# Second expert part of a three-part kernel: its ScalarE, VectorE and GpSimd operations in a written-out order, transposes into tiles of their own, low products of an output later

## The chip, the cores and the metric

The kernel runs on one core of one Trainium2 chip. The metric is the device time of one execution in microseconds (us). The profile gives times from the start of its own span, which is some 2 us shorter than the device time of the same execution.

## The reference

A linear attention with decay feeds two dense expert layers; the second one has a softmax and a layer norm inside. The part that the change touches is the second layer.

```
attn_out = _attn_ref(q, k, v)                 # (4, 8, 768, 64), decayed running state
x = attn_out as (3072 tokens, 512)
# first expert layer, d_ff = 2048
h = x @ w_in;  g = h - tanh(h);  x = g @ w_out
# second expert layer, d_ff = 1024
h = x @ w_in2
e = exp(h - max(h));  sm = e / (sum(e) + 1e-9)
solu = h * sm
mu = mean(solu);  var = mean((solu - mu)**2)
ln = (solu - mu) / sqrt(var + 1e-6) * g_ln
out = ln @ w_out2
```

## The kernel before

All matrix products are made in a high and a low part: an operand is cast to a reduced format (the high part), the rest (the low part) is a difference, and TensorE multiplies high by high, high by low and low by high. So each operand costs a cast on ScalarE (L160) and a difference on VectorE or GpSimd (L161, L475).

Tokens are handled in tiles of 128. The second layer takes 12 pairs of tiles, `Pair(0)` to `Pair(11)`; tile `2j+1` is called a here and tile `2j` b. A pair's first product is made with seven block products instead of eight, in the order P1, P2, P6, P5, P7, P4, P3 (`Pair.part`), each of 6 matmuls (L925). Between them ScalarE copies partial sums out of PSUM (`keep2`, L932, tiles `part`); P6 and P7 go on in the bank of P1 and so wait for the copy before them. VectorE makes the halves of a tile's hidden row from a bank and a copy, with a running maximum (`add_half`, L940): a's are complete after P4, b's after P3.

Then each tile goes through `soft`: exp on ScalarE (L950), weighting with the hidden row and its sum on VectorE (L952, called weigh here; the mean is a small operation behind it, L953), subtraction of the mean on ScalarE (L954, center), squares on ScalarE (L956), a transpose in 32x32 blocks on VectorE (L958), and small operations for the scale (L961 to L967, the last two on GpSimd). The transposed tile is written to DRAM (`ud`, L959) and read back in another order into `hn` (L972, `turn`); so the transpose across partitions is completed. `trans` splits that tile into `uh` and `ul` (L160, L161). `outp` makes the second product, 24 matmuls (L989) of `uh` and `ul` with the eight decoded pieces of w_out2, and evicts it with the scale (L993).

In the last stretch `pair_of(j, j-1)` makes pair j's seven products, and `outs(j-1)` the two outputs of the pair before it. Pair 10 has no outputs behind it: pair 11 follows at once, then the outputs of pairs 9, 10 and 11. Pair 0's products lie between the last products of the first layer (`products_y`, L377, 12 matmuls for each of 16 steps f; the operands of step f are `gp`, split by `split_p(f)` with L160 and L161); pair 0's P3 comes behind step 11, and steps 12 to 15 follow it. This place is called the changeover here.

Who sets the order: TensorE's instructions stand as the program writes them (`tc.manual_schedule`). Those of ScalarE, VectorE and GpSimd are placed by the scheduler of the framework, which also puts in the semaphores; `pin` keeps an instruction in the order of the program. SP's loads of `hn` and writes of `ud` are pinned. Tiles of 4 KB a partition come from one pool of 40 (`t4`); the transpose is written over `ex`.

Of the kernel before, what the change touches and what calls it, by code (L numbers as in the profile page):

```python
# [47 lines left out]
LATER = 3  # L48
LOADS = 3
# [39 lines left out]
def body(ctx: ExitStack, tc, z, w_in, w_out, w_in2, w_out2, g_ln, cst, tab, out):  # L89
# [67 lines left out]
    P1, P2, P6, P5, P7, P4, P3 = range(7)  # L157

    def parts(h, o, src, eng):
        nc.scalar.copy(h, src)  # L160
        eng.tensor_tensor(o, src, h.bitcast(F32), ALU.subtract)  # L161
# [309 lines left out]
    def on_pool(n, out, a, b, op):  # L471
        k = out.shape[1] // n
        for i in range(n):
            at = slice(i * k, (i + 1) * k)
            nc.gpsimd.tensor_tensor(out[:, at], a[:, at], b[:, at], op)  # L475

    def sum_y(j):
        t = yl[j]
        a11, a12, a21, a22 = (t[:, i, k : k + 2, :] for i in range(2) for k in (0, 2))
        s = ysum[j] = t4([P, 4, 2, P], F32, "ysum")  # L480
        s1, s2, s3, s4 = (s[:, i, :, :] for i in range(4))
        nc.gpsimd.tensor_tensor(s1, a21, a22, ALU.add)
        nc.gpsimd.tensor_tensor(s2, s1, a11, ALU.subtract)
        nc.gpsimd.tensor_tensor(s3, a11, a21, ALU.subtract)
        nc.gpsimd.tensor_tensor(s4, a12, s2, ALU.subtract)

    def split_y(j, halves=(0, 1)):
        flat = "p a k t -> p (a k t)"
        for g in halves:
# [11 lines left out]
            for lo, n, src in todo:  # L501
                h, o = (w[:, lo : lo + n, :, :].rearrange(flat) for w in y)
                nc.scalar.copy(h, src)  # L503
                on_pool(n, o, src, h.bitcast(F32), ALU.subtract)
# [425 lines left out]
    def keep2(ph):  # L930
        t = t2([P, 512], F32, "part")
        nc.scalar.copy(t, ph)  # L932
        return t
# [4 lines left out]
    def add_half(h, half, ph, part, seen):  # L938
        hn, nm = h
        nc.vector.tensor_tensor_reduce(  # L940
            hn[:, half * 512 : (half + 1) * 512], ph, part, -1.0,
            3.0e38 if seen is None else nm[seen], ALU.add, ALU.min, nm[half],
        )

    def soft(i, h, last):

        hn, nmx = h[0], h[1][last]
        ex = t4([P, FF2], F32, "ex")
        ssum = sp.tile([P, 1], F32, tag="ssum", name="ssum")
        nc.scalar.activation(ex, hn, AF.Exp, bias=nmx, scale=-1.0, accum_out=ssum)  # L950
        us = sp.tile([P, 1], F32, tag="us", name="us")
        nc.vector.scalar_tensor_tensor(ex, hn, 1.0, ex, ALU.mult, ALU.mult, accum_out=us)  # L952
        nc.vector.tensor_scalar(us, us, -1.0 / FF2, None, ALU.mult)  # L953
        nc.scalar.activation(hn, ex, AF.Identity, bias=us)  # L954
        ssq = sp.tile([P, 1], F32, tag="ssq", name="ssq")
        nc.scalar.activation(ex, ex, AF.Square, bias=us, accum_out=ssq)  # L956

        nc.vector.transpose(ex, hn)  # L958
        pin(nc.sync.dma_start(out=ud[i], in_=ex))  # L959

        nc.vector.tensor_scalar(ssum, ssum, 1e-9, -1.0, ALU.add, ALU.mult)  # L961
        nc.vector.reciprocal(ssum, ssum)
        nc.vector.tensor_scalar(ssq, ssq, ssum, ssum, ALU.mult, ALU.mult)
        nc.vector.tensor_scalar(ssq, ssq, 1.0 / FF2, 1e-6, ALU.mult, ALU.add)
        sc = sp.tile([P, 1], F32, tag="sc", name="sc")
        nc.gpsimd.tensor_tensor(sc, ssq, mhalf, ALU.pow)
        nc.gpsimd.tensor_tensor(sc, sc, ssum, ALU.mult)  # L967
        uc[i], sc2[i] = hn, sc
# [8 lines left out]
    def trans(i):  # L977
        u = uc.pop(i)
        uh, ul = (t4([P, NF2 * P], F32R, "u" + n) for n in "hl")
        parts(uh, ul, u, nc.vector)  # L980
        ut[i] = [w.rearrange("p (f t) -> p f t", f=NF2) for w in (uh, ul)]

    def outp(i):
        uh, ul = ut.pop(i)
        po = ps_o.tile([P, DM], F32, tag="o", name="po")
        for f in range(NF2):
            bh, bl = dec2.w[f]
            for n, (a, b) in enumerate(((uh, bh), (uh, bl), (ul, bh))):
                nc.tensor.matmul(  # L989
                    po, a[:, f, :], b, start=f == 0 and n == 0, stop=f == NF2 - 1 and n == 2  # L990
                )
        ob = t2([P, DM], F32, "ob")
        nc.scalar.activation(ob, po, AF.Copy, scale=sc2.pop(i))  # L993
        at = i % B * S + i // B * P
        nc.scalar.dma_start(out=out[at : at + P, :], in_=ob)

    class Pair:
# [5 lines left out]
        def part(self, m):  # L1003
# [20 lines left out]
            elif m == P4:  # L1024
# [3 lines left out]
                soft(2 * j + 1, self.a, 0)  # L1028
            else:
                product2(j, P3, self.q3, False)  # L1030
                add_half(self.b, 1, self.q3, self.u2, 0)
                soft(2 * j, self.b, 1)
# [6 lines left out]
    for n, (s, f) in enumerate(steps):  # L1039
# [19 lines left out]
        if s == NSB - 1:  # L1059
# [13 lines left out]
            for m in {8: (P1, P2), 9: (P6, P5), 10: (P7, P4), 11: (P3,)}.get(f, ()):  # L1073
                pair.part(m)
            if f == 9:
# [15 lines left out]
    def pair_of(j, before):  # L1091
        pair = Pair(j)
        for n, m in enumerate((P1, P2, P6, P5, P7, P4, P3)):
            if n == 5 and before is not None:
                trans(2 * before + 1)
            pair.part(m)
            if n in (0, 2) and j + 1 < NJ:
                split_y(j + 1, (n // 2,))
            if n == 4 and j + 2 < NJ:
                sum_y(j + 2)  # L1100
            if n == 4 and j + 3 < NJ:
                load_y(j + 3)
        turn(j)
        if before is not None:
            trans(2 * before)

    def outs(j, after=None):
        for half in (1, 0):
            outp(2 * j + half)
            if after is not None:  # L1110
                trans(2 * after + half)

    with tc.manual_schedule(engines={mybir.EngineType.PE}):
        for j in range(1, NJ - 1):
            pair_of(j, j - 1)
            if j < NJ - 2:
                outs(j - 1)
        pair_of(NJ - 1, None)
        outs(NJ - 3, NJ - 2)
        outs(NJ - 2, NJ - 1)  # L1120
# [60 lines left out]
```

## Time and profile before

| | |
|---|---|
| median of 3 executions | 853.78 us (853.65 to 854.4) |
| profiled execution, its own time | 853.42 us |
| its span | 851.5 us |
| share of the span that matmuls are busy | 96% |
| share that VectorE, ScalarE, GpSimd are busy | 63%, 55%, 34% |

The time is the median of the unprofiled executions; the profile shows one execution more, which took 853.42 us. Shares are of the whole span, over stages that have different limits; what an edit is worth has to be read in its own stage.

### The profile page before, as it was taken

To read this page: it belongs to the slowest core of one execution; us is meant where nothing else is said; L and a number is where in the kernel's file an instruction comes from. 1 tells how busy PE (TensorE), PEld (TensorE's weight loads), DVE (VectorE), ACT (ScalarE), POOL (GpSimd) and SP (SyncE) were. 2 spreads that over 40 slices of the span, in tenths; PEclk is the share of its full clock that TensorE was granted. 3 is DMA by queue.
4 is the path that set the end of the run, shared out by engine and by line. 5 is a ranking of instruction groups with operands and counts; after the bars stand their busy time and mean duration, and the time that the engine had idled before them with its cause. 6 is when DMAs were issued, how large, how long until landed. Compare 5 with 4: busy or idle time off the path is not lost.

```text
span 851.5 us, 16381 instructions
## 1 busy us (share of the span) xinstructions
PE 820.1 (96%) x6296; PEld 672.9 (79%) x6296; DVE 536.0 (63%) x999; ACT 468.2 (55%) x880; POOL 291.2 (34%) x304
## 2 busy tenths in 40 slices
PE   5699999999999999999999999999999999999998
PEld 4678888788877777888788888888888888888876
DVE  3778985999867948322662897483555555555561
ACT  4546753656456546444562446354666666666672
POOL 4511200090635329344400260064444444444310
PEclk8899999999999999999999999999999999999999
DMA  9658854353899825963592818380787667776675
GB/s 359 248 205 292 289 201 129 123 183 108 308 366 329 301 77 175 399 263 128 196 366 94 313 44 309 112 283 26 149 173 149 149 149 148 149 149 123 124 173 99
DMA packets 168461, 169.42 MB, mean 199 GB/s; under 512 B 105664, under 2 KB 117952, under 8 KB 168384
## 3 DMA queue, kind: packets, MB, share of 16 engines
q1 hardware_dynamic: 160032, 153.38, 59.5%
q10 hardware_dynamic: 8352, 15.00, 4.9%
q8 instruction: 49, 0.80, 0.4%
q14 instruction: 28, 0.23, 0.1%
HBM read 107.02 MB, written 61.34 MB: 198 GB/s over the span
## 4 chain that ended last, share of the span: by engine, by line
PE 84%; DVE 5%; DMA 4%; issue 3%; ACT 2%; POOL 1%; SPq 0%; ACTq 0%; DVEq 0%; POOLq 0%
PE py L377 30%; PE ph L753 16%; PE po L989 14%; PE ph L352 10%; PE ph L925 10%; PE out L228 3%; PE sc L228 2%; DVE ul L161 1%; DMA z<-z 1%; DVE hn L940 1%; DMA raw<-w_in 1%; DMA wcd<-wch 1%; ACT part L932 1%; DMA hn<-ud 1%; POOL hs L771 0%
## 5 line engine op out<-in xcount | busy, mean ns | idle before, releaser
L377 PE MATMUL py<-gp,w 128*128 128x512 f32 x768 | 175.1, 389 | 0.0
L377 PEld LDWEIGHTS py<-gp,w 128*128 128x128 f32 x768 | 144.1, 188 | 30.0
L989 PE MATMUL po<-w,uh 128*128 128x512 f32 x384 | 118.5, 390 | 0.0
L771 POOL TENSOR_TENSOR hs<-hs,th 128x512 f32<-128x512 f32 x48 | 66.5, 1389 | 96.1 <-ACT th L769 84.0
L989 PEld LDWEIGHTS po<-w,uh 128*128 128x128 f32 x384 | 72.1, 188 | 14.8
L352 PE MATMUL ph<-xh,w 128*128 128x512 f32 x256 | 83.1, 399 | 0.0
L377 PE MATMUL py<-gh,w 128*128 128x512 f32 x256 | 79.2, 390 | 0.3 <-ACT gh L365 0.3
L989 PE MATMUL po<-w,ul 128*128 128x512 f32 x192 | 75.9, 395 | 2.9 <-DVE ul L161 2.5
L153 ACT CAST w<-wf 128x512 fp32r<-128x512 f32 x70 | 43.1, 621 | 55.9 <-DVE wf L144 46.1
L940 DVE CUSTOM_DVE_ANT_0 hn<-ph,part 128x512 f32<-128x512 f32 x24 | 16.6, 691 | 82.0 <-ACT part L932 46.8
L769 ACT ACTIVATE th<-hs 128x512 f32<-128x512 f32 x48 | 30.3, 631 | 61.5 <-DVE hs L779 54.9
L154 DVE TENSOR_TENSOR w<-wf,w 128x512 fp32r<-128x512 f32 x70 | 51.1, 734 | 14.4 <-ACT w L153 13.6
L161 DVE TENSOR_TENSOR gp<-g,gp 128x512 fp32r<-128x512 f32 x64 | 48.2, 764 | 18.5 <-ACT gp L160 18.4
L925 PE MATMUL ph<-w,yhs 128*128 128x512 f32 x192 | 59.2, 390 | 0.2 <-ACT part L932 0.2
L753 PE MATMUL ph<-xh,wch 128*128 128x512 f32 x140 | 57.1, 408 | 1.6 <-DVE hs L779 1.6
L352 PEld LDWEIGHTS ph<-xh,w 128*128 128x128 f32 x256 | 48.6, 190 | 11.1 <-DVE w L154 0.4
L377 PEld LDWEIGHTS py<-gh,w 128*128 128x128 f32 x256 | 48.0, 188 | 10.6 <-ACT gh L365 0.7
L160 ACT CAST gp<-g 128x512 fp32r<-128x512 f32 x64 | 38.6, 618 | 30.8 <-DMA g<-gd 18.4
L753 PE MATMUL ph<-xl,wch 128*128 128x512 f32 x140 | 55.3, 395 | 0.0
L779 DVE TENSOR_TENSOR hs<-ph,part 128x512 f32<-128x512 f32 x48 | 32.9, 686 | 35.3 <-PE ph L753 22.9
L753 PE MATMUL ph<-xh,wcl 128*128 128x512 f32 x140 | 55.1, 394 | 0.0
L475 POOL TENSOR_TENSOR yla<-yl,yha 128x256 fp32r<-128x256 f32 x36 | 27.7, 797 | 78.7 <-ACT yha L503 78.7
(123 smaller groups left out, 1788.0 us busy)
## 6 DMA issues: line engine op xcount, KB each, us to landing
z<-z SPq DMA_DIRECT2D x48, 512.0 KB, 6.5
g<-gd SPq DMA_DIRECT2D x64, 256.0 KB, 5.3
raw<-w_in SPq DMA_DIRECT2D x24, 512.0 KB, 6.7
raw<-w_out SPq DMA_DIRECT2D x24, 512.0 KB, 4.5
gd<-hs SPq DMA_DIRECT2D x48, 256.0 KB, 3.5
ud<-ex SPq DMA_DIRECT2D x24, 512.0 KB, 3.1
hn<-ud SPq DMA_DIRECT2D x24, 512.0 KB, 6.9
y1d<-ysb SPq DMA_DIRECT2D x24, 256.0 KB, 3.6
```

Source lines behind the costliest of these rows:

```text
L153: pin(nc.scalar.copy(hi, wf), fixed)
L154: pin(eng.tensor_tensor(lo, wf, hi.bitcast(F32), ALU.subtract), fixed)
L160: nc.scalar.copy(h, src)
L161: eng.tensor_tensor(o, src, h.bitcast(F32), ALU.subtract)
L228: pin(nc.tensor.matmul(o, a, b, start=True, stop=True, skip_group_check=True), held[0])
L352: nc.tensor.matmul(ph, a[:, k, :], x, start=n == 0, stop=n == 3 * NK - 1), s < 2
L377: nc.tensor.matmul(py[e], a[:, cols], x, start=f == 0 and n == 0, stop=f == NF1 - 1 and n == 2)
L753: nc.tensor.matmul(ph, a, x, start=first and n == 0, stop=n == 5, skip_group_check=True)
L771: eng.tensor_tensor(g, h, th, ALU.subtract)
L779: nc.vector.tensor_tensor(h, ph, part, ALU.add)
L925: nc.tensor.matmul(ph, x[:, r, :], w, start=first and n == 0, stop=n == 5, skip_group_check=True)
L989: nc.tensor.matmul(po, a[:, f, :], b, start=f == 0 and n == 0, stop=f == NF2 - 1 and n == 2)
```

## The change

`fix` pins an instruction from the place on where `late[0]` is set, ahead of pair 1: from there on the operations of ScalarE, VectorE and GpSimd in the second layer stand as the program writes them. `soft` is cut into five steps (`Soft`), which `pair_of` and `outs` call at chosen places. The transpose goes into a tile of its own, `ut`. `trans` is cut into `high` (cast) and `low` (difference). In `outp` the low product of piece f comes `LAG` = 3 pieces later. The last output is evicted in two halves, one on ScalarE and one on VectorE, with two stores.

```
 LATER = 3
+LAG = 3
...
+    late = [False]
+
+    def fix(ins):
+        pin(ins, late[0])
...
+    class Soft:
+
+        def __init__(self, i, h, last):
+            self.i, self.hn, self.nm = i, h[0], h[1][last]
+
+        def exp(self):
...
+        def weigh(self):
...
+        def center(self):
+            fix(nc.scalar.activation(self.hn, self.ex, AF.Identity, bias=self.us))
+
+        def turn(self):
+            t = t4([P, FF2], F32, "ut")
+            fix(nc.vector.transpose(t, self.hn))
+            pin(nc.sync.dma_start(out=ud[self.i], in_=t))
+            uc[self.i] = self.hn
+
+        def norm(self):
+            ssq, ssum = sp.tile([P, 1], F32, tag="ssq", name="ssq"), self.ssum
+            fix(nc.scalar.activation(self.ex, self.ex, AF.Square, bias=self.us, accum_out=ssq))
...
-        for f in range(NF2):
-            bh, bl = dec2.w[f]
-            for n, (a, b) in enumerate(((uh, bh), (uh, bl), (ul, bh))):
...
+        todo = []
+        for f in range(NF2 + LAG):
+            if f < NF2:
+                todo += [(uh, f, 0), (uh, f, 1)]
+            if f >= LAG:
+                todo.append((ul, f - LAG, 0))
...
+        if i == NTT - 2:
+            l, r = slice(0, DM // 2), slice(DM // 2, DM)
+            fix(nc.scalar.activation(ob[:, l], po[:, l], AF.Copy, scale=sc))
+            fix(nc.vector.tensor_scalar(ob[:, r], po[:, r], sc, None, ALU.mult))
...
+                if m in (P4, P3):
+                    u = pair.sa if m == P4 else pair.sb
+                    u.weigh()
+                    u.center()
+                    u.turn()
+                    u.norm()
...
-    def pair_of(j, before):
+    def pair_of(j, before=None):
+
+        a, b = (None, None) if before is None else (2 * before + 1, 2 * before)
         pair = Pair(j)
         for n, m in enumerate((P1, P2, P6, P5, P7, P4, P3)):
-            if n == 5 and before is not None:
-                trans(2 * before + 1)
             pair.part(m)
-            if n in (0, 2) and j + 1 < NJ:
-                split_y(j + 1, (n // 2,))
...
+            if n < 2 and j + 1 < NJ:
+                split_y(j + 1, (n,))
+            if n == 2 and a is not None and j > 1:
+                high(a)
+                low(a)
+            if n == 4:
+                if a is not None:
+                    if j > 1:
+                        high(b)
+                    else:
+                        high(a)
+                        low(a)
...
+        for u in (pair.sa, pair.sb):
+            u.weigh()
+        if a is not None and j == 1:
+            high(b)
+        pair.sa.center()
+        pair.sa.turn()
+        if a is not None:
+            low(b)
+        pair.sb.center()
+        pair.sb.turn()
         turn(j)
...
+    late[0] = True
     with tc.manual_schedule(engines={mybir.EngineType.PE}):
...
+        for j in range(1, NJ - 2):
+            pair = pair_of(j, j - 1)
+            outs(j - 1, pair)
+        pair = pair_of(NJ - 2, NJ - 3)
+        pair.sa.norm()
+        pair.sb.norm()
+        pair = pair_of(NJ - 1)
+        outs(NJ - 3, pair, NJ - 2)
+        outs(NJ - 2, None, NJ - 1)
         outs(NJ - 1)
```

What the built programs hold at three places follows (line numbers are each program's own).

ScalarE at the changeover, from pair 0's first exp on: before, `gp` being the casts of steps 13, 14 and 15 of the first layer.

```order
L950 ACTIVATE ex,ssum<-hn,nm 128x1024
L160 CAST gp<-g 128x512
L954 ACTIVATE hn<-ex,us 128x1024
L950 ACTIVATE ex,ssum<-hn,nm 128x1024
L160 CAST gp<-g 128x512 x2
L153 CAST w<-wf 128x512
```

The same place in the change.

```order
L958 ACTIVATE ex,ssum<-hn,nm 128x1024
L970 ACTIVATE hn<-ex,us 128x1024
L980 ACTIVATE ex,ssq<-ex,us 128x1024
L165 CAST gp<-g 128x512
L958 ACTIVATE ex,ssum<-hn,nm 128x1024
L970 ACTIVATE hn<-ex,us 128x1024
L980 ACTIVATE ex,ssq<-ex,us 128x1024
L165 CAST gp<-g 128x512 x2
L154 CAST w<-wf 128x512
```

Tile a's center and squares now stand ahead of the cast of step 13, and tile b's exp, center and squares ahead of those of steps 14 and 15. On VectorE each difference `gp` stands behind the same tile's transpose and scale operations; before, it stood ahead of them.

VectorE in a pair of the middle, from the addition of tile a's first half on: before (`ISA hn` are the additions, `ul` the low products of the pair before).

```order
L940 ISA hn,nm<-ph_7212,part,nm 128x512
L940 ISA nm 128x1
L161 TENSOR_TENSOR ul<-hn,uh 128x1024
L940 ISA hn,nm<-ph_7183,part,nm 128x512
L940 ISA nm 128x1
L952 SCALAR_TENSOR_TENSOR ex,us<-hn,ex 128x1024
```

The same pair in the change, from one addition earlier.

```order
L1003 TENSOR_TENSOR ul<-hn,uh 128x1024
L945 ISA hn,nm<-ph_7148,part 128x512
L945 ISA nm 128x1
L945 ISA hn,nm<-ph_7219,part,nm 128x512
L945 ISA nm 128x1
L945 ISA hn,nm<-ph_7191,part,nm 128x512
L945 ISA nm 128x1
L964 SCALAR_TENSOR_TENSOR ex,us<-hn,ex 128x1024
L967 TENSOR_SCALAR us<-us 128x1
```

The low product of tile a moved from behind the third addition to ahead of the second; that of tile b now stands between the two transposes, where before it followed the second weigh.

ScalarE from pair 10's first exp to pair 11's copies: before (`part` are pair 11's copies of P1, P6, P5 and P7).

```order
L950 ACTIVATE ex,ssum<-hn,nm 128x1024
L932 COPY part<-ph_8762 128x512
L950 ACTIVATE ex,ssum<-hn,nm 128x1024
L160 CAST uh<-hn 128x1024
L954 ACTIVATE hn<-ex,us 128x1024
L932 COPY part<-ph_8762 128x512
L956 ACTIVATE ex,ssq<-ex,us 128x1024
L932 COPY part<-ph_8787 128x512
```

The same place in the change.

```order
L958 ACTIVATE ex,ssum<-hn,nm 128x1024 x2
L970 ACTIVATE hn<-ex,us 128x1024 x2
L980 ACTIVATE ex,ssq<-ex,us 128x1024 x2
L937 COPY part<-ph_8784 128x512 x2
L937 COPY part<-ph_8809 128x512
```

The copy of pair 11's P1, which stood between pair 10's two exps, now stands behind both exps, both centers and both squares.

## Rows read from the trace of the kernel before

**Rows 1.** Page, part 1: busy time, share of the span, instructions.

```profile
PE 820.1 (96%) x6296; PEld 672.9 (79%) x6296; DVE 536.0 (63%) x999; ACT 468.2 (55%) x880; POOL 291.2 (34%) x304
```

**Rows 2.** Waits of TensorE from 430 us on: total us, times, longest.

```profile
PE po L989 <- DVE ul L161: 2.5, 9, 0.3
...
PE ph L925 <- ACT part L932: 0.2, 1, 0.2
```

**Rows 3.** Timeline of TensorE, steps 12 to 15 and pair 1's start.

```profile
594.67 11.04 PE L377 MATMUL py<-gp,w 128*128 128x512 f32 x48
605.55 0.61 PE L925 MATMUL ph<-w,yha 128*128 128x512 f32 x2
```

**Rows 4.** Timeline of TensorE, first and last of nine such waits.

```profile
615.97 0.50 PE L989 MATMUL po<-w,ul 128*128 128x512 f32 x1 [0.28 <-DVE ul L161]
...
783.87 0.50 PE L989 MATMUL po<-w,ul 128*128 128x512 f32 x1 [0.28 <-DVE ul L161]
```

**Rows 5.** Timeline of TensorE: pair 11's start, pair 9's outputs, the last matmul.

```profile
803.95 0.62 PE L925 MATMUL ph<-w,yha 128*128 128x512 f32 x2
...
813.97 0.61 PE L989 MATMUL po<-w,uh 128*128 128x512 f32 x2
...
847.15 0.39 PE L989 MATMUL po<-w,ul 128*128 128x512 f32 x1
```

**Rows 6.** Timeline of VectorE, a low product in a middle pair.

```profile
677.61 1.22 DVE L161 TENSOR_TENSOR ul<-hn,uh 128x1024 fp32r<-128x1024 f32 x1
```

**Rows 7.** Timeline of ScalarE at the changeover: start, duration, instruction, idle before.

```profile
591.69 1.15 ACT L950 ACTIVATE ex<-hn,nm 128x1024 f32<-128x1024 f32 x1 [1.67 <-DVE nm L940]
...
592.84 0.61 ACT L160 CAST gp<-g 128x512 fp32r<-128x512 f32 x1
595.02 1.15 ACT L954 ACTIVATE hn<-ex,us 128x1024 f32<-128x1024 f32 x1 [1.58 <-DVE ssum L962]
596.08 1.14 ACT L950 ACTIVATE ex<-hn,nm 128x1024 f32<-128x1024 f32 x1
...
599.59 1.15 ACT L956 ACTIVATE ex<-ex,us 128x1024 f32<-128x1024 f32 x1
```

**Rows 8.** Timeline of VectorE at the changeover.

```profile
592.97 1.22 DVE L952 SCALAR_TENSOR_TENSOR ex<-hn,ex 128x1024 f32<-128x1024 f32 x1 [1.31 <-ACT ex L950]
...
594.18 0.68 DVE L161 TENSOR_TENSOR gp<-g,gp 128x512 fp32r<-128x512 f32 x1
594.78 0.15 DVE L953 TENSOR_SCALAR us<-us 128x1 f32<-128x1 f32 x1
...
594.92 0.73 DVE L940 CUSTOM_DVE_ANT_0 hn<-ph,part,nm 128x512 f32<-128x512 f32 x1
...
603.18 1.25 DVE L958 STREAM_TRANSPOSE ex<-hn 128x1024 f32<-128x1024 f32 x1 [0.69 <-ACT ex L956]
```

**Rows 9.** Timeline of ScalarE, pair 10's first exp and pair 11's first copy.

```profile
803.69 1.16 ACT L950 ACTIVATE ex<-hn,nm 128x1024 f32<-128x1024 f32 x1 [0.72 <-DVE nm L940]
...
805.51 0.59 ACT L932 COPY part<-ph 128x512 f32<-128x512 f32 x1 [0.58 <-PE ph L925]
```

**Rows 10.** Timeline of TensorE behind two idle times in the first layer.

```profile
298.96 1.52 PE L228 MATMUL sc<-vq,z 64*64 64x64 f32 x64 [2.84 <-POOL hs L771]
...
336.45 0.50 PE L753 MATMUL ph<-xh,wch 128*128 128x512 f32 x1 [1.63 <-DVE hs L779]
```

**Rows 11.** Windows behind them: length, busy us (count) by engine, granted clock, DMA.

```profile
300.50:303.90 3.40, 3.40 (x8) 2.69 (x9) 1.03 (x3) 1.07 (x3) 1.28 (x1) 0.50 0.22 82
...
336.50:340.00 3.50, 3.50 (x15) 2.88 (x16) 2.11 (x2) 1.92 (x4) 2.97 (x3) 1.00 0.99 362
```

**Rows 12.** Page, part 6: issues, count, size, median us from issue to landing.

```profile
ud<-ex SPq DMA_DIRECT2D x24, 512.0 KB, 3.1
hn<-ud SPq DMA_DIRECT2D x24, 512.0 KB, 6.9
```

**Rows 13.** Timeline of ScalarE, the last eviction.

```profile
847.63 0.69 ACT L993 ACTIVATE ob<-po,sc 128x512 f32<-128x512 f32 x1 [4.75 <-PE po L989]
```

More of the change, by code (lines that the diff above doesn't have):

```diff
@@ L931, in keep2 @@
         t = t2([P, 512], F32, "part")
-        nc.scalar.copy(t, ph)
+        fix(nc.scalar.copy(t, ph))
         return t
@@ L939, in add_half @@
         hn, nm = h
-        nc.vector.tensor_tensor_reduce(
+        fix(nc.vector.tensor_tensor_reduce(
             hn[:, half * 512 : (half + 1) * 512], ph, part, -1.0,
             3.0e38 if seen is None else nm[seen], ALU.add, ALU.min, nm[half],
[L943 to L968, printed above, removed]
@@ L975, in turn, with high, low @@
             ))
[L977 to L981, printed above, removed]
+    def high(i):
+        uh, ul = ut[i] = [t4([P, NF2 * P], F32R, "u" + n) for n in "hl"]
+        fix(nc.scalar.copy(uh, uc[i]))
+    def low(i):
+        uh, ul = ut[i]
+        fix(nc.vector.tensor_tensor(ul, uc.pop(i), uh.bitcast(F32), ALU.subtract))
     def outp(i):
[L984 removed]
+        uh, ul = (w.rearrange("p (f t) -> p f t", f=NF2) for w in ut.pop(i))
         po = ps_o.tile([P, DM], F32, tag="o", name="po")
[L986 to L991 removed]
+        todo = []
[4 more added lines that the diff above has]
+                todo.append((ul, f - LAG, 0))
+        for n, (a, f, lo) in enumerate(todo):
+            nc.tensor.matmul(
+                po, a[:, f, :], dec2.w[f][lo], start=n == 0, stop=n == len(todo) - 1
+            )
         ob = t2([P, DM], F32, "ob")
[L993 removed]
         at = i % B * S + i // B * P
[L995 removed]
+        sc = sc2.pop(i)
+        if i == NTT - 2:
+            l, r = slice(0, DM // 2), slice(DM // 2, DM)
+            fix(nc.scalar.activation(ob[:, l], po[:, l], AF.Copy, scale=sc))
+            fix(nc.vector.tensor_scalar(ob[:, r], po[:, r], sc, None, ALU.mult))
+            nc.scalar.dma_start(out=out[at : at + P, l], in_=ob[:, l])
+            nc.sync.dma_start(out=out[at : at + P, r], in_=ob[:, r])
+            return
+        fix(nc.scalar.activation(ob, po, AF.Copy, scale=sc))
+        fix(nc.scalar.dma_start(out=out[at : at + P, :], in_=ob))
     class Pair:
@@ L1103, in pair_of, with outs @@
         turn(j)
-        if before is not None:
-            trans(2 * before)
-    def outs(j, after=None):
+        return pair
+    def outs(j, of=None, after=None):
         for half in (1, 0):
+            if of is not None:
+                (of.sa if half else of.sb).norm()
             outp(2 * j + half)
             if after is not None:
-                trans(2 * after + half)
+                high(2 * after + half)
+                low(2 * after + half)
+    late[0] = True
     with tc.manual_schedule(engines={mybir.EngineType.PE}):
[L1114 to L1120, printed above, removed]
+        for j in range(1, NJ - 2):
[7 more added lines that the diff above has]
+        outs(NJ - 2, None, NJ - 1)
```

49 lines of the change are left out of this document (35 added, 14 removed).

## The prediction

> **What bounds the kernel now.** I read the page first, then TensorE's waits, then timelines. Matmuls are busy 96% of the span, the other engines 34 to 63% [rows 1]. A busy share can flatter a pipelined engine, so I look at starts: steps 12 to 15 and what follows begin 48 matmuls in 605.55 - 594.67 = 10.88 us, 0.2267 us each, with no gap [rows 3]. From pair 1's start to the last matmul stand 11 x 42 + 24 x 24 = 1038 matmuls; 1037 spacings make 235.1 us, the trace takes 847.15 - 605.55 = 241.6 [rows 3, 5]. So the last stretch can give back 6.5 us at most, 0.8% of the time, and whatever newly stops TensorE there is added whole.
>
> Where the 6.5 lie: nine times a low product `ul` of tile a comes late [rows 2, 4]. The period of these waits is (783.87 - 615.97) / 8 = 20.99 us; 90 matmuls need 20.40; each costs 0.59, together 5.3. Pair 11's 42 matmuls take 813.97 - 803.95 = 10.02 against 9.52 and lose 0.5, at a copy [rows 2, 5]. The 143 spacings from pair 9's first output to the last matmul take 33.18 against 32.41, 0.8 lost [rows 5].
>
> **Middle pairs.** I count from a pair's first matmul; a product takes 6 x 0.2267 = 1.36. Pair 11 starts at 803.95, so pair 10 at 794.43, and its exp of a at 803.69 [rows 9], which is 9.26: P4's matmuls end their issue at 8.16, then comes the addition (0.73 [rows 8]). The low product of a now stands ahead of the second addition: copies of P6's bank until 4.9, cast of `uh` (an estimate: 1.05, between the 0.61 of 512 columns and twice that [rows 7]) until 5.9, `ul` 1.22 [rows 6] until 7.1. Outputs start at 9.52 and with the lag need it eight matmuls later, at 11.3. Tile b: weigh a follows exp a and the addition of b, 10.5 to 11.7, weigh b 11.85 to 13.1, center a meanwhile 11.9 to 13.05, transpose a (1.25) to 14.5, then `ul` of b to 15.7 [rows 6 to 8]; it is wanted at 9.52 + 5.44 + 1.81 = 16.8. Both are in time. The reread tiles too: the write lands in 3.1, the read in 6.9 [rows 12]; transpose a ends at 14.5, b at 16.8, so they land about 4.1 and 6.4 into the next pair, where their casts stand at 4.8 and 7.5. Pairs 2 to 9 thus lose their wait: -8 x 0.59 = **-4.7** (0 if the margin of 1.1 us were eaten up).
>
> **Pair 1** is different: there `high(a)` stays behind P7, and `ul` of a moved ahead of the third addition. Cast 7.5 to 8.6, `ul` to 9.8, so exp a starts at 10.6 instead of 9.26; everything behind slips by 1.3, the cast of b comes ahead of center a, and `ul` of b ends near 17.5 instead of 16.8. A wait of 0.9 with the restart takes the place of 0.59: **+0.3** (0 to +0.6).
>
> **The changeover.** TensorE starts step 13 at 594.67 + 2.72 = 597.39, step 14 at 600.11 and step 15 at 602.83. ScalarE takes its row in order. Exp a ends 592.84; weigh a 592.97 to 594.19, mean to 594.35 [rows 7, 8]. Center a 594.4 to 595.55; squares to 596.6 (each starts 0.09 before the one ahead of it ends, 596.08 against 595.02 + 1.15); cast of step 13 to 597.2. Its difference (0.68) waits for the squares' small operations (estimate: two of 0.15 to 0.2) and ends near 598.0. Step 13's first matmul runs, the second, wanted at 597.62, waits until 598.05 and restarts slowly: +0.5. Exp b comes behind that cast: 597.15 to 598.3. Weigh b 598.45 to 599.65, mean 599.8; center b 599.9 to 601.0; squares to 602.1; only now the cast of step 14, to 602.7. TensorE wants it at 600.6: +2.1. Its difference stands behind transpose b and the small operations, 602.75 to 603.45, for a matmul wanted at 603.0: +0.6 with the restart. Step 15 finds all it needs. Before, the same casts ran at 592.84 and 597.2 and hid in ScalarE's idle 1.67 and 1.58 us [rows 7]; that cover is gone. Sum **+3.3** (2.9 to 3.6): pair 1 starts at 608.8 instead of 605.55. Nothing behind wins it back, since the stretch is TensorE's own work.
>
> **Pair 10 to pair 11.** Before, ScalarE copied pair 11's P1 at 805.51, between pair 10's exps [rows 9], and P6, wanted at 12.24 (806.67), did not wait. Now that copy stands behind both exps, centers and squares. Exp a 9.26 to 10.4, exp b (its addition ends 10.5) to 11.7, center a 11.9 to 13.05, center b (mean of b at 13.2) 13.25 to 14.4, squares to 15.55 and 16.7, copy (0.59) to 17.3. P6 goes on at 17.35: a wait of 5.1, 5.2 with the restart. If center b waited for nothing, six operations at a spacing of 1.06 would still put the copy at 16.2 and the wait at 4.0: bounds 4.0 to 5.3. Queued behind the copy are P6's, P5's and P7's copies; these then come in time, each product lasting 1.36. Less the 0.5 of before: **+4.7**.
>
> **Last outputs.** Transposes no longer wait for the squares to leave `ex`, so `hn` of pairs 10 and 11 lands earlier, and pair 9 to 11's outputs (32.6 us of matmuls) cover the rest: **-0.8** (0 to -0.8). The last eviction takes 0.69 [rows 13]; its halves stand on two engines, but in the built program VectorE's half waits for ScalarE's. Two times about 0.45 is 0.2 more, a store half as long 0.2 less: **0** (-0.35 to +0.3).
>
> **The clock.** After an idle time of 2.84 us TensorE's granted clock went to 0.50, its lower level of 1.2 GHz, for 3.4 us; after one of 1.63 us it stayed at 1.00 [rows 10, 11]. In 3.4 us at the lower level 8 matmuls started, where 15 do at the upper: 7 x 0.227 = 1.6 lost. Pair 11's idle time is about 5.0 us, well beyond 2.84: **+1.6** (0 to 2.4, if it falls for one stretch and a part). The changeover's longest is about 1.95, nearer to 1.63: 0, with 1.6 as the other end.
>
> **Sum**: -4.7 + 0.3 + 3.3 + 4.7 - 0.8 + 0 + 1.6 = +4.4 on the execution's own 853.42, 857.8. The median stands 0.36 above that execution: **858.2 us**. Other edits cost nothing: the lag adds no matmul, SP's one more store comes at the end, and semaphore waits of 0.02 us lie in idle time.
>
> **A rule against this sum.** The Trainium skill, page "Perfetto Trace Analysis", section "Identifying the Most-Contended Engine", says that matmul busy time is a poor measure of TensorE's headroom and the busy share of weight loads a better one. That share is 79% here. By the rule a fifth of the time would be in reserve, and new waits could be caught up; the sum would then be -6.5, 847.3 us. The trace disagrees in this stretch: starts never come closer than 0.227 us, whatever waited before them.
>
> **Rivals.** (1) As summed, 858.2: chance 0.52. (2) The clock falls at the changeover too: its waits of 2.1 and 0.6 lie close together. 859.8: 0.20. (3) The clock falls nowhere: 856.6: 0.10. (4) GpSimd's differences and sums, which before ran mostly ahead of the low products, now lie beside `ul` of a and perhaps weigh a. No row prices that; if VectorE slows by more than the margin of 1.1 us, a wait of up to 0.3 comes back in eight pairs: 860.6: 0.07. (5) The changeover's wait does not come, because casts get through earlier than I place them: 858.2 - 3.3 = 854.9, no change. The order of ScalarE speaks against it: 0.06. (6) Faster: TensorE catches up behind a wait. It decides if matmuls can start closer than 0.227 us; then all waits vanish in the reserve, 847.3. Rows 3 speak against it: 0.05.
>
> Differences under 0.2% (1.7 us) can't be told from no change here. Faster 0.05, same 0.06, slower 0.89. Cases 1 to 3 with the bounds of their terms give 856 to 860.5 as the likeliest's own range; with cases 4 and 5 the range is 855.0 to 861.0.
>
> **What would show it.** Right: no wait for `ul` in pairs 2 to 9 and a period of 20.4; steps 13 and 14 waiting for `gp`, pair 1 starting 3.3 later; P6 of pair 11 waiting 5 us for `part`, with a granted clock of 0.50 behind it. Wrong: waits of TensorE for `ul` of b or `uh` in the middle pairs (the margins of 1.1 and 0.7 us), or copies of pair 11 that come before the squares.

## The result

The change is slower. Six executions took 860.44 us in the median (858.59 to 864.85) beside 853.71 us (853.28 to 855.69) for the kernel before on the same chip, a ratio of 1.0083 with a 95% interval of 1.0055 to 1.0111. The forecast was 858.2 us, in a range of 855.0 to 861.0. Four of the six executions lie in that range and two above it (863.17 and 864.85).

The profiled execution of the change, the longest of the six, took 864.85 us, with a span of 863.1. To see where that went, I cut both profiles at the same matmuls of TensorE: the first one of step 12, of pair 1, of pair 2, of pairs 10 and 11, of pair 9's outputs, and the last one. Each number is the difference of two such starts in us; "end" runs from the last matmul to the end of the span.

| stretch | before | change | difference | forecast |
|---|---|---|---|---|
| steps 12 to 15 (changeover) | 10.88 | 15.99 | +5.11 | +3.3 |
| pair 1 and outputs 0 | 20.97 | 21.60 | +0.63 | +0.3 |
| pairs 2 to 9, outputs 1 to 8 | 167.91 | 163.20 | -4.71 | -4.7 |
| pair 10 | 9.52 | 9.52 | 0 | 0 |
| pair 11 | 10.01 | 17.50 | +7.49 | +6.3 (4.7 and 1.6 of clock) |
| outputs 9 to 11 | 33.18 | 32.41 | -0.77 | -0.8 |
| end | 4.33 | 4.29 | -0.04 | 0 |
| sum | 256.80 | 264.51 | +7.71 | +4.4 |

Up to 8.6 us ahead of step 12 ScalarE, VectorE and GpSimd run the same instructions in the same order in both profiles, and yet step 12 starts 3.88 us later in the change: 598.55 in the rows below, 594.67 in [rows 3]. All of it has come about by 434 us. A part of it are waits for which the profile names no releaser, as these two on TensorE's timeline (start, duration, instruction, idle before), which the kernel before does not have at these places.

```profile
107.55 0.46 PE L233 MATMUL sc<-vs,z 64*64 64x64 f32 x16 [1.31 <-issue]
263.80 0.39 PE L758 MATMUL ph<-xh,wcl 128*128 128x512 f32 x1 [1.10 <-issue]
```

In the eleven profiles of this study, whose edits all lie behind that place, step 12 starts between 591.55 and 598.91 us. So much of what separates single executions can lie ahead of the change, and each edit is judged here by the stretches of the table first and by the median second.

### The profile page after: what moved, and what is told of

The parts are those of the page before. It is cut to its first block, busy times and chain, and to the rows that moved or that the text cites. A ratio compares the mean times of both kernels' runs of the same rounds, so it can differ in the third digit from the quotient of the medians.

```text
span 863.1 us, 16439 instructions
## 1 busy us (share of the span) xinstructions
PE 823.6 (95%) x6296; PEld 676.4 (78%) x6296; DVE 551.9 (64%) x1000; ACT 470.7 (55%) x880; POOL 309.0 (36%) x304
## 4 chain that ended last, share of the span: by engine, by line
PE 72%; DVE 11%; DMA 6%; issue 5%; ACT 4%; POOL 1%; SPq 1%; ACTq 0%; DVEq 0%; POOLq 0%
PE py L382 20%; PE po L1015 14%; PE ph L758 13%; PE ph L930 12%; PE ph L357 8%; DMA z<-z 3%; PE out L233 2%; PE sc L233 2%; DVE gl L373 1%; DVE wf L142 1%; DVE wf L145 1%; DVE w L155 1%; DMA raw<-w_in 1%; DMA gd<-hs 1%; DVE wf L139 1%
## 5 line engine op out<-in xcount | busy, mean ns | idle before, releaser
L382 PE MATMUL py<-gp,w 128*128 128x512 f32 x768 | 177.7, 392 | 2.5 <-ACT gp L165 2.1
L1015 PE MATMUL po<-w,uh 128*128 128x512 f32 x384 | 106.6, 389 | 0.0
L930 PE MATMUL ph<-w,yhs 128*128 128x512 f32 x192 | 61.4, 402 | 4.9 <-ACT part L937 4.9
L1015 PE MATMUL po<-w,ul 128*128 128x512 f32 x192 | 63.1, 390 | 0.9 <-DVE ul L1003 0.9
L382 PEld LDWEIGHTS py<-gh,w 128*128 128x128 f32 x256 | 48.0, 188 | 10.6 <-ACT gh L370 0.7
L758 PE MATMUL ph<-xh,wc 128*128 128x512 f32 x168 | 52.8, 390 | 0.3 <-ACT part L768 0.3
```

Of the source, the lines that this page charges most:

```text
L382: nc.tensor.matmul(py[e], a[:, cols], x, start=f == 0 and n == 0, stop=f == NF1 - 1 and n == 2)
L758: nc.tensor.matmul(ph, a, x, start=first and n == 0, stop=n == 5, skip_group_check=True)
L930: nc.tensor.matmul(ph, x[:, r, :], w, start=first and n == 0, stop=n == 5, skip_group_check=True)
L1015: nc.tensor.matmul(po, a[:, f, :], dec2.w[f][lo], start=n == 0, stop=n == len(todo) - 1)
```

## The profile after

All waits of TensorE from 586 us on, in the profile of the change: total us, times, longest. They answer to [rows 2].

```profile
PE ph L930 <- ACT part L937: 4.9, 1, 4.9
PE py L382 <- ACT gp L165: 2.1, 1, 2.1
PE po L1015 <- DVE ul L1003: 0.9, 1, 0.9
PE py L382 <- DVE gp L166: 0.4, 2, 0.2
```

The nine waits for `ul` have become one. In their place stand a wait for the copy `part` and three for `gp`. TensorE's timeline at the changeover and at pair 11, the same places as in [rows 3, 5]:

```profile
598.55 3.30 PE L382 MATMUL py<-gp,w 128*128 128x512 f32 x13
602.07 2.83 PE L382 MATMUL py<-gp,w 128*128 128x512 f32 x11 [0.23 <-DVE gp L166]
606.97 0.51 PE L382 MATMUL py<-gp,w 128*128 128x512 f32 x1 [2.06 <-ACT gp L165]
607.69 7.01 PE L382 MATMUL py<-gp,w 128*128 128x512 f32 x23 [0.22 <-DVE gp L166]
614.54 0.62 PE L930 MATMUL ph<-w,yha 128*128 128x512 f32 x2
...
811.35 0.39 PE L930 MATMUL ph<-w,yla 128*128 128x512 f32 x1
816.65 1.22 PE L930 MATMUL ph<-w,yhs 128*128 128x512 f32 x2 [4.91 <-ACT part L937]
```

Before, the 48 matmuls of steps 12 to 15 were one row without a gap. Now they are four rows: step 13 stops at its second matmul, step 14 at its first and its second. The last of them is 7.01 us long for 23 matmuls, where 5.2 are needed. The granted clock, the share of full speed that the profile shows for TensorE, tells why. Windows behind the two long idle times: length, busy us (count) of PE, PEld, DVE, ACT, POOL, granted clock, DMA.

```profile
607.69:611.12 3.43, 3.43 (x9) 2.71 (x10) 1.69 (x2) 0.27 (x1) 1.73 (x3) 0.53 1.24 217
816.65:822.70 6.05, 6.05 (x15) 4.75 (x16) 1.51 (x8) 1.11 (x2) 0.74 (x2) 0.51 1.30 197
```

At the lower of its two levels (1.2 GHz, granted clock 0.5) TensorE starts a matmul every 0.427 us instead of 0.227. It stayed there for some 3.4 us behind the changeover's waits and some 6 us behind pair 11's.

ScalarE's timeline at the changeover shows what the casts stood behind. It answers to [rows 7].

```profile
595.57 1.15 ACT L958 ACTIVATE ex<-hn,nm 128x1024 f32<-128x1024 f32 x1 [1.67 <-DVE nm L945]
...
598.35 1.15 ACT L970 ACTIVATE hn<-ex,us 128x1024 f32<-128x1024 f32 x1 [1.55 <-DVE ssum L982]
599.54 1.15 ACT L980 ACTIVATE ex<-ex,us 128x1024 f32<-128x1024 f32 x1
...
600.69 0.61 ACT L165 CAST gp<-g 128x512 fp32r<-128x512 f32 x1
601.20 1.15 ACT L958 ACTIVATE ex<-hn,nm 128x1024 f32<-128x1024 f32 x1
...
603.98 1.15 ACT L970 ACTIVATE hn<-ex,us 128x1024 f32<-128x1024 f32 x1 [1.55 <-DVE ssum L982]
605.17 1.15 ACT L980 ACTIVATE ex<-ex,us 128x1024 f32<-128x1024 f32 x1
...
606.31 1.12 ACT L165 CAST gp<-g 128x512 fp32r<-128x512 f32 x2
```

The cast of step 13 begins 5.12 us after exp a; in [rows 7] it followed at 1.15. ScalarE was idle 1.55 us twice, with the cast ready and standing behind center. The cast of step 14 starts at 606.31, and 0.66 us later TensorE starts that step.

ScalarE at pair 10's end and pair 11's start, which answers to [rows 9]:

```profile
808.60 1.15 ACT L958 ACTIVATE ex<-hn,nm 128x1024 f32<-128x1024 f32 x1 [0.28 <-DVE nm L945]
...
809.91 1.15 ACT L958 ACTIVATE ex<-hn,nm 128x1024 f32<-128x1024 f32 x1
...
811.39 1.15 ACT L970 ACTIVATE hn<-ex,us 128x1024 f32<-128x1024 f32 x1 [0.23 <-DVE us L967]
812.72 1.15 ACT L970 ACTIVATE hn<-ex,us 128x1024 f32<-128x1024 f32 x1 [0.18 <-DVE us L967]
813.77 1.13 ACT L980 ACTIVATE ex<-ex,us 128x1024 f32<-128x1024 f32 x1
...
814.90 1.13 ACT L980 ACTIVATE ex<-ex,us 128x1024 f32<-128x1024 f32 x1
...
816.03 0.56 ACT L937 COPY part<-ph 128x512 f32<-128x512 f32 x1
```

Six operations of pair 10, and then the copy on which P6 of pair 11 has been waiting: it ends at 816.59, P6 goes on at 816.65. Pair 10 starts at 799.34, so exp a stands at 9.26 and the copy ends at 17.25; the forecast had 9.26 and 17.3.

## Experiments

The runs are given by their stretches, cut as in the table above, from one profile each; a ratio compares medians on one chip. "Sum" is from step 12 to the end, to be held against 256.80 of the kernel before and 264.51 of the change. Pair 10 takes 9.52 in all of them.

| run | 12 to 15 | pair 1, out 0 | 2 to 9 | 11 | out 9 to 11 | end | sum | ratio to before, 95% |
|---|---|---|---|---|---|---|---|---|
| squares of pair 10 later | 14.51 | 21.59 | 163.20 | 12.48 | 32.41 | 4.28 | 257.99 | 1.0042 (1.0024 to 1.0060) |
| pair 10 spread | 15.87 | 21.60 | 163.20 | 9.76 | 32.41 | 4.29 | 256.65 | 0.9996 (0.9974 to 1.0018) |
| changeover mended | 10.88 | 21.61 | 163.20 | 16.89 | 32.41 | 4.28 | 258.79 | 1.0011 (0.9991 to 1.0031) |
| before with the lag alone | 10.88 | 20.40 | 163.91 | 10.01 | 32.51 | 4.34 | 251.57 | 0.9943 (0.9921 to 0.9965) |
| change without the lag | 15.99 | 22.99 | 170.49 | 16.58 | 32.41 | 4.29 | 272.27 | 1.0197 (1.0165 to 1.0229) |
| three places mended | 10.88 | 20.40 | 163.20 | 9.76 | 32.41 | 4.28 | 250.45 | 0.9916 (0.9889 to 0.9944) |
| before with own tiles alone | 16.09 | 29.72 | 232.35 | 9.52 | 42.14 | 4.52 | 343.86 | one execution, 943.03 us |
| change again | 14.51 | 21.59 | 163.20 | 17.31 | 32.41 | 4.28 | 262.82 | one execution, 858.73 us |
| mended, halves apart | 10.88 | 20.40 | 163.20 | 9.76 | 32.41 | 4.28 | 250.45 | one execution, 851.17 us |

**The squares of pair 10 later.** Is the wait of P6 set by what stands ahead of the copy on ScalarE? Only the squares and the small operations of `norm` move; `then` is called behind P7's copy.

```
+                if then is not None:
+                    then()
...
-        pair.sa.norm()
-        pair.sb.norm()
-        pair = pair_of(NJ - 1)
+        ten = pair
+
+        def then():
+            ten.sa.norm()
+            ten.sb.norm()
+
+        pair = pair_of(NJ - 1, None, then)
```

> Theory (ScalarE's queue makes P6 of pair 11 wait): only the two squares of pair 10 and the small operations behind them move, to behind pair 11's copy of P7; both centers still stand ahead of the copy of P1. In the profile of the change the second center ends at 813.87 and the copy at 816.59 held P6 until 816.65. So the copy ends 2.25 us earlier and the wait of P6 shrinks from 5.07 to about 2.8. It stays near the 2.84 us behind which the first layer's clock fell, so the clock still falls for some 3 us of time, of which 0.9 to 3.1 us are lost. Median about 858 (860.4 less 2.3). Rival A (the clock does not fall behind 2.8 us here): 855 to 856. Rival B (the wait comes from something else than the queue, say the copy's own bank): no change, 860.4.

TensorE's timeline at P6, and the window behind it:

```profile
810.45 0.72 PE L930 MATMUL ph<-w,yhs 128*128 128x512 f32 x2 [2.65 <-ACT part L937]
```

```profile
810.45:813.50 3.05, 3.05 (x13) 2.54 (x14) 2.28 (x4) 0.59 (x1) 0.00 (x0) 1.00 0.61 244
```

The spacing at P6 went from 5.30 to 3.04 us, the 2.25 us that the two squares take: the queue is the cause, and rival B falls. On the clock the theory was wrong in this execution. It stayed at 1.00, as rival A said, and pair 11 takes 12.48 = 9.52 + 2.81 of wait + 0.15 of restart. (By restart I mean that behind a wait the second matmul comes later than usual: the two at 810.45 last 0.72 us together, where 0.61 is usual.) The median, 857.94, is the theory's and not the rival's. For the other executions there is only a mean granted clock of the whole span (0.986 to 0.994, the profiled one 0.988), which does not tell in which stage it fell, so what they add to the profiled one is not shown.

**Pair 10 spread between pair 11's copies.**

```
+            if ten is not None:
+                if n == 0:
+                    ten.sa.center()
+                    ten.sa.turn()
+                    low(2 * NJ - 6)
+                if n == 2:
+                    ten.sb.center()
+                    ten.sb.turn()
+                    turn(NJ - 2)
+                if n == 4:
+                    ten.sa.norm()
+                    ten.sb.norm()
...
+        if j == NJ - 2:
+            return pair
...
-        pair.sa.norm()
-        pair.sb.norm()
-        pair = pair_of(NJ - 1)
+        pair = pair_of(NJ - 1, None, pair)
```

`low(2 * NJ - 6)` is the low product of pair 9's tile b.

> Theory: pair 10's centers, transposes, squares are spread between pair 11's copies, in the order exp a, exp b, copy P1, center a, copy P6, center b, copies P5 and P7, squares. The copy of P1 then follows exp b at once and ends near its due time; P6 waits at most 0.2, and with no idle time the clock stays at 1.00. Gain against the change: 5.07 wait + 3.1 clock - 0.2 = 8.0 us, median about 852.5; the changeover's waits stay. Rival: the wait only moves, to P7 behind the copy of P6 or to the outputs of pair 9, whose low product of tile b stands on VectorE between the transposes: then a wait of 1 us or more shows there and the gain is under 7 us.

P6 on TensorE's timeline has no idle time left that the profile shows:

```profile
804.23 0.39 PE L930 MATMUL ph<-w,yla 128*128 128x512 f32 x1
804.56 0.73 PE L930 MATMUL ph<-w,yhs 128*128 128x512 f32 x2
```

Its spacing is 0.33 us instead of 0.227. Pair 11 takes 9.76, 7.74 less than in the change, and the median (853.69) can't be told from that of the kernel before on the same chip (854.03). Theory held, with 7.74 for the forecast 8.0. The rival's wait at P7 or at pair 9's outputs did not come: outputs 9 to 11 take 32.41 as in the change.

**The changeover mended.**

```
-                    u.center()
-                    u.turn()
-                    u.norm()
+            if f == 11:
+                pair.sa.center()
+                pair.sa.turn()
+            if f == 12:
+                pair.sb.center()
+                pair.sb.turn()
...
+            if f == 13:
+                pair.sa.norm()
+                pair.sb.norm()
```

> Theory (casts of gp behind pair 0's operations): pair 0's center, transpose and squares are written later, so that the cast of step 13 stands between exp a and center a, that of step 14 behind squares a, that of step 15 behind squares b. No wait of step 13 and 14 for gp, pair 1 starts 5.0 us earlier relative to step 12 (3.4 of waits, 1.6 of the lower clock). Pair 11 is left as it is. Median about 855.4. Rival: the granted clock at the changeover falls for another reason than the idle time: then 857, with a granted clock near 0.5 and no wait ahead of it. Second rival: step 14 is now late by its difference behind weigh b, 0.5 us or more.

TensorE's timeline of steps 12 to 15 is one row again, as in [rows 3]:

```profile
595.00 11.04 PE L382 MATMUL py<-gp,w 128*128 128x512 f32 x48
605.88 0.61 PE L930 MATMUL ph<-w,yha 128*128 128x512 f32 x2
```

All 5.11 us are gone, the clock's part with the waits. Neither rival held. The sum is 1.99 above that of the kernel before: pair 11's wait and pair 1's, less what the middle pairs and the last outputs gain. The median, 855.08, was forecast at 855.4 and can't be told from that of the kernel before (854.03).

**The kernel before with the lag alone.**

```
+LAG = 3
...
-        for f in range(NF2):
-            bh, bl = dec2.w[f]
-            for n, (a, b) in enumerate(((uh, bh), (uh, bl), (ul, bh))):
...
+        todo = []
+        for f in range(NF2 + LAG):
+            if f < NF2:
+                todo += [(uh, f, 0), (uh, f, 1)]
+            if f >= LAG:
+                todo.append((ul, f - LAG, 0))
...
```

> The kernel before with the low products of an output three pieces later and nothing else. Theory (the nine waits for ul are short ones that the lag alone covers): 9 x 0.55 = 5.0 us less than before, 848.7, a period of 20.4 us in pairs 1 to 9, and no other wait of TensorE changed. The written-out order would then have been needed for none of the gain. Rival (the lag alone moves the wait to tile b's low product, or the order that ScalarE gets from it delays the centers): gain under 2.5 us.

From 586 us on one wait of TensorE is left that the view names, that of pair 11 in [rows 2]:

```profile
PE ph L926 <- ACT part L933: 0.2, 1, 0.2
```

Pairs 1 to 9 take 184.31 us instead of 188.88, and the outputs at the end 32.51 instead of 33.18: 5.24 of the change's possible gain come from these few lines, which write out no order of ScalarE or VectorE. Pairs 2 to 9 still lose 0.71, most of it in two short waits for a cast `uh`, which the theory did not have. Otherwise it held; the median is 849.53 where 848.7 was forecast.

**The change without the lag.**

```
-LAG = 3
+LAG = 0
```

> The change with the low products of an output in their old place (LAG = 0); ScalarE, VectorE and GpSimd stand as in the change. Theory (the earlier place of tile a's low product took its wait away, the lag was not needed for it): in pairs 2 to 9 ul of a ends some 2 us before it is wanted, and no wait for it comes back. Tile b's ul, which stands behind transpose a, ended 15.7 us after the pair's start in the trace of the change (pair 4) and would now be wanted at 9.52 + 5.44 + 0.45 = 15.4, so a wait of 0.3 to 0.6 with the restart stands at each second output: 8 x 0.45 = 3.6 us more over pairs 2 to 9, and in pair 1 the wait of 1.17 grows by 1.4. Sum about 5 us more than the change. Rival (the lag did it all): the waits for ul of a come back, 8 x 0.55 = 4.4, and none for b. Second rival (neither mattered): 163.2 us for pairs 2 to 9 as in the change.

Waits of TensorE for `ul` in this run, and the one of pair 2 in the timeline:

```profile
PE po L1015 <- DVE ul L1003: 6.7, 10, 1.8
```

```profile
649.64 0.50 PE L1015 MATMUL po<-w,ul 128*128 128x512 f32 x1 [0.59 <-DVE ul L1003]
```

One wait in each of pairs 2 to 9, each at the second output, and none for tile a there: so the earlier place of a's low product does take a's wait away, as the theory says. But b's wait is (170.49 - 163.20) / 8 = 0.91 us and not 0.45, because b's `ul` ends later than the expectation placed it: it gives 15.7 as read in the trace, and the trace shows 16.48 (below). Pair 1 grew by 1.39 as forecast, and the sum by 7.76 instead of some 5.

**All three places mended.** The edits of the runs "pair 10 spread" and "changeover mended", and pair 1 treated like every other pair; this is the edit for pair 1.

```
-            if n == 2 and a is not None and j > 1:
+            if n == 2 and a is not None:
                 high(a)
                 low(a)
...
-                    if j > 1:
-                        high(b)
-                    else:
-                        high(a)
-                        low(a)
+                    high(b)
...
-        if a is not None and j == 1:
-            high(b)
```

> The change with all three places mended: pair 0's steps around the casts of gp, pair 10's between pair 11's copies, and pair 1's high and low products of tile a behind P6 as in every other pair. Theory (the three places are all that the change lost, and they are independent): from step 12 to the last matmul 10.88 + 20.40 + 163.2 + 9.52 + 9.75 + 32.41 = 246.2 us, against 260.2 in the profile of the change and 252.5 before; a median 6.3 under before's, 847 to 848. Rival: pair 0's reread tile comes too late for the early cast in pair 1, and ScalarE, held in order, is late for P7 there: a wait of 1 us or more in pair 1.

From step 12 to the last matmul it takes 246.17, the forecast 246.2, and the view of waits names none. The median is 847.56 beside 854.41, 0.84% less than before (0.56 to 1.11). The interval overlaps that of the lag alone (0.35 to 0.79 less); that this kernel is the faster of the two rests on the stretches, 250.45 against 251.57. The changeover and pair 11 take here what they took when each was mended alone, so those two losses are independent; pair 1 was mended only together with them. Together the three are all that the change lost but for 0.24, P6's spacing in pair 11.

**The kernel before with the transposes in tiles of their own.**

```
-        nc.vector.transpose(ex, hn)
-        pin(nc.sync.dma_start(out=ud[i], in_=ex))
+        t = t4([P, FF2], F32, "ut")
+        nc.vector.transpose(t, hn)
+        pin(nc.sync.dma_start(out=ud[i], in_=t))
```

> The kernel before with the transposes in tiles of their own and nothing else: the scheduler still places the operations. In its built order pair 0's center and squares now stand ahead of the cast of step 13, as in the change, and in every middle pair the cast of uh of tile b stands behind the eviction of tile a's output, a center and squares. Theory 1 (the changeover's loss comes from this edit and not from the written-out order): steps 12 to 15 take 10.88 + 3.4 us, or 5 with the lower clock. Theory 2 (with own tiles the written-out order is needed): output b waits for uh from 15.0 to about 19.3 us after a pair's start, some 4.3 us in each of pairs 1 to 9, 39 us in all and more where the clock falls: 895 to 915. Rival: the transposes being free of the squares is all that matters, steps 12 to 15 take 10.88 and the time is 853.

Waits of TensorE from 585 us on, and ScalarE in pair 1 from the eviction to the cast:

```profile
PE po L990 <- ACT uh L160: 53.9, 10, 7.0
...
PE py L377 <- ACT gp L160: 2.1, 1, 2.1
PE py L377 <- DVE gp L161: 0.5, 2, 0.2
```

```profile
629.25 0.67 ACT L994 ACTIVATE ob<-po,sc 128x512 f32<-128x512 f32 x1
...
630.83 1.15 ACT L954 ACTIVATE hn<-ex,us 128x1024 f32<-128x1024 f32 x1 [0.92 <-DVE us L953]
632.01 1.15 ACT L956 ACTIVATE ex<-ex,us 128x1024 f32<-128x1024 f32 x1
...
633.15 1.03 ACT L160 CAST uh<-hn 128x1024 fp32r<-128x1024 f32 x1
```

Both theories held in the place of the waits. The changeover's 2.1 and the small waits for `gp` appear with this edit alone, with nothing written out by hand: steps 12 to 15 take 16.09. And in the middle pairs the cast waits behind the eviction of the output before it. Its size was off: 5.3 us a pair, and the clock falls behind each, so each of pairs 2 to 9 takes 8.06 us more than in the kernel before, and the time is 943.03, beyond the forecast 895 to 915. The outputs at the end lose too, 42.14 against 33.18.

**The change once more.** No edit.

> The change once more, unaltered: what differs between executions. Theory: waits of TensorE from step 12 on repeat within 0.1 us (pair 1 to output 0: 21.60, pairs 2 to 9: 163.20), while the time behind them in which the clock is at its lower level differs (changeover 0 to 1.6 us lost, pair 11 up to 3.1), and the stages ahead of step 12 differ by up to 5 us. Rival: the waits themselves differ by more than 0.5 us, so that the spread of the times comes from them.

The waits repeat: TensorE's timeline gives the same idle times, and pairs 2 to 9 the same 163.20. The clock doesn't. Windows at the places that the change's windows show:

```profile
603.26:606.70 3.44, 3.44 (x15) 2.85 (x16) 1.70 (x2) 0.27 (x1) 1.75 (x3) 1.00 1.24 217
810.73:816.40 5.67, 5.67 (x14) 4.47 (x15) 1.50 (x8) 0.73 (x2) 0.74 (x2) 0.51 1.28 200
```

Here the changeover takes 14.51, 3.63 more than before, and all of that is waits, since the clock stayed at 1.00; behind pair 11's wait it fell as in the first profile. Step 12 started at 594.11, 4.44 us earlier than in the change's first profile, and the execution took 858.73 us, within 0.6 of the forecast for the median. Theory held, the rival fell.

**The halves of the last output apart.**

```
-            fix(nc.vector.tensor_scalar(ob[:, r], po[:, r], sc, None, ALU.mult))
+            ob2 = t2([P, DM // 2], F32, "ob2")
+            fix(nc.vector.tensor_scalar(ob2, po[:, r], sc, None, ALU.mult))
...
-            nc.sync.dma_start(out=out[at : at + P, r], in_=ob[:, r])
+            nc.sync.dma_start(out=out[at : at + P, r], in_=ob2)
...
```

The three mended places are in this kernel too.

> The three mended places, and the right half of the last output in a tile of its own (128x256), so that VectorE's half no longer shares a tile with ScalarE's. Theory (in the change VectorE's half waited for ScalarE's because both write one tile): the two halves start together, 0.48 us after the last matmul; from the last matmul to the end 3.8 us instead of 4.28. Rival: the end hangs on ScalarE's store alone, and the stretch stays at 4.28.

VectorE's half in the change, and then in this run:

```profile
859.76 0.48 DVE L1024 TENSOR_SCALAR ob<-po,sc 128x256 f32<-128x256 f32 x1 [7.98 <-ACT ob L1023]
```

```profile
846.08 0.48 DVE L1025 TENSOR_SCALAR ob<-po,sc 128x256 f32<-128x256 f32 x1 [7.98 <-ACT ob L1023]
```

Nothing moved, and my theory falls: the tile that both wrote was not what orders them. Both still read one bank, `po`. The Trainium skill, page "PSUM — Partial Sum Buffer", section "PSUM bank collisions raise a hardware error ⚠️", says that two engines must not read one bank at once and that the compiler's scheduler adds a dependency for it; the trace agrees with such a dependency, but two banks were not tried, so this cause stays argued.

## Why the prediction was right, and where it was off

**Middle pairs: right in size, thinner than argued.** -4.71 against -4.7. Edits of the change do it together: the written order, which was run only with the transposes' own tiles, takes away tile a's wait, and the lag keeps tile b's from coming. The lag alone would have done nearly as much. The margin of b was overstated. I placed the reread tile of b at 6.4 us into the pair and its `ul` at an end of 15.7, 1.1 us early. In pair 4 of the change, which starts at 676.94, ScalarE and VectorE have:

```profile
686.08 1.05 ACT L999 CAST uh<-hn 128x1024 fp32r<-128x1024 f32 x1 [1.56 <-DMA hn<-ud]
687.04 1.15 ACT L958 ACTIVATE ex<-hn,nm 128x1024 f32<-128x1024 f32 x1
```

```profile
692.24 1.18 DVE L1003 TENSOR_TENSOR ul<-hn,uh 128x1024 fp32r<-128x1024 f32 x1
```

The tile lands at 9.1, the cast waits 1.56 us for it, and exp a stands behind that cast in the written order. The tile is late for the most part because its reread took 8.5 us from issue to landing, and that of tile a 6.4, where I had put the median of [rows 12], 6.9, for both. So exp a starts at 10.1 instead of 9.26, and `ul` of b ends at 16.48 where it is wanted at 16.8: 0.3 to spare and not 1.1. The number held, then, by less than the forecast said. Without the lag the same lateness is the 0.91 us a pair of the fifth run.

**Pair 1: +0.63 against +0.3.** The mechanism was right, `ul` of b late behind a slip of everything. The size is off because `ul` of tile a took 1.69 us and not 1.22, so that exp a starts 11.03 us into the pair and not 10.6:

```profile
623.11 1.69 DVE L1003 TENSOR_TENSOR ul<-hn,uh 128x1024 fp32r<-128x1024 f32 x1 [0.25 <-ACT uh L999]
```

**Changeover: waits right, clock wrong.** Without the clock the stretch takes 14.51, +3.63 against +3.3 (whose three terms, 0.5, 2.1 and 0.6, add up to 3.2). I took 0 for the clock, and 1.6 as the other end. It fell in four of the six profiled executions that had these waits (15.87 to 16.09) and not in two (14.51). What decides it is not shown. Rival 2 (859.8) has the mechanism of the profiled execution. Nor did I see the cause: by the seventh run the order that I blamed comes with the transposes' own tiles. With that edit alone the scheduler places center and squares ahead of the casts; why it does is not shown.

**Pair 11: wait right to 0.1, clock mis-sized.** P6 waited 5.07 us and 0.11 of restart followed, less the 0.49 of before: +4.7. (The view puts the idle time at 4.91; 5.07 is the spacing of P6's first matmul, 816.65 - 811.35, less the usual 0.23.) The term of the clock was 1.6; four profiles with this wait take 16.58 to 17.50, which is 1.9 to 2.8 above the 14.7 without it. I had scaled one stretch of 3.4 us from [rows 11], and here the clock stayed low for 4 to 6.

**Last outputs: -0.77 against -0.8,** but the reason given does not carry it alone. With the lag and the old tiles the stretch takes 32.51, so the lag alone is nearly enough. With own tiles and the written order but no lag it takes 32.41. Own tiles alone, the reason that I gave, take 42.14 when the scheduler places the operations: they are not enough.

**The end:** 0, and VectorE's half did wait, as said.

**Rivals.** That TensorE catches up (847.3) fell: 720 matmuls of pairs 2 to 9 take 163.20 us, 0.2267 each, in every profile of the written order with the lag, whatever waited before. By the rule of the Trainium skill, page "Perfetto Trace Analysis", section "Identifying the Most-Contended Engine", the 78% of weight loads would have left a reserve; the trace shows none. Rival 4, VectorE slower beside GpSimd, exists but stays inside the margin in pairs 2 to 9 (next section but one); in pair 1 it makes the miss of 0.3. The miss of 3.3 us in the sum is 1.5 of clock and 0.3 of waits at the changeover, 0.3 in pair 1 and 1.2 of clock in pair 11. The measured difference of the medians, +6.7, lies between the two sums seen, +6.0 without the changeover's clock (262.82) and +7.7 with it. That it lies in the stated range is partly luck: with the clock as in the profiled execution the sum gives 853.78 + 7.71 = 861.5, above the range.

## What to carry to other kernels

When an order changes, whether by hand or because the scheduler is given another choice, list for each engine what the last instruction of the old stage stands ahead of in the new one: the steady loop kept its promise here to 0.01 us, and both losses came at the two ends, where a cast or a copy of the next stage stood behind a whole tile's chain. Try the smallest edit alone first, since the lag by itself gave 5.2 of the 6.4 us that the mended order gives, and look at the built order after a tile is freed, since that alone moved the casts. A long wait on TensorE can cost more than itself: behind 5 us of it another 1.9 to 2.8 us were lost at half the clock.

## What the runs showed of the hardware

**The clock behind the same wait differs from execution to execution.** Behind 5 us of idle time it fell in four of four, and cost 1.9 to 2.8 us. Behind 2.65 us in pair 11 it did not fall in one execution. In the first layer all eleven profiles have the wait of [rows 10], 2.80 to 2.84 us; the clock fell there in ten of them and not in that of "pair 10 spread", whose window behind it is the following. So [rows 11], on which the prediction's clock terms rest, showed one execution and not a rule.

```profile
297.58:304.00 6.42, 6.37 (x144) 5.21 (x145) 2.73 (x7) 2.94 (x6) 1.30 (x1) 1.00 0.34 125
```

Behind the changeover's waits (2.06, with 0.23 and 0.22 around it) it fell in four of six.

**VectorE and GpSimd hinder each other.** The same low product in windows of pair 4 of the change, tile a and tile b:

```profile
682.78:684.31 1.53, 1.53 (x8) 1.26 (x8) 1.52 (x1) 0.83 (x2) 1.53 (x2) 1.00 1.46 171
692.24:693.42 1.18, 1.18 (x7) 0.98 (x6) 1.18 (x3) 1.18 (x4) 0.00 (x0) 1.00 0.24 97
```

Beside GpSimd's operations on 128x256 it takes 1.52 us, with GpSimd idle 1.18. So it is in all eight profiles of the written order: 1.48 to 1.70 us ten times in each, and 1.18 to 1.23 the other fourteen. GpSimd pays too: on its timeline in pair 1, beside the `ul` that starts at 623.11,

```profile
622.99 0.73 POOL L488 TENSOR_TENSOR ysum<-ysum,yl 128x256 f32<-128x256 f32 x1
623.68 1.72 POOL L489 TENSOR_TENSOR ysum<-yl 128x256 f32<-128x256 f32 x1
```

one operation of 0.73 us becomes 1.72. Where GpSimd's operation is short and starts second, GpSimd alone pays. In "before with own tiles alone" a low product that starts at 634.21 keeps its 1.23 us, and this operation of GpSimd, 0.19 us where nothing of VectorE stands beside it, takes 0.97:

```profile
634.51 0.97 POOL L968 TENSOR_TENSOR sc<-sc,ssum 128x1 f32<-128x1 f32 x1
```

The Trainium skill, page "SBUF — State Buffer", section "Who interferes with whom", says that a VectorE instruction with two inputs in that memory contends with a GpSimd instruction that reads there, over a pair of ports that the two engines share, and that this is an exclusive lock. The trace agrees in size: the 0.99 us that GpSimd's operation lost is most of a low product's 1.18, and the low product's own 0.34 to 0.51 is part of one operation of GpSimd. That it is these ports and not something else, no run separates.
